# A recurrent memory kernel: the new memory summed over bands once, turned by a VectorE block transpose, its rows moved by DMA

## The chip, the cores and the metric

The kernel runs on one core of a Trainium2 chip. The metric is the device time of one execution in microseconds, lower is better; before the change three runs gave 1661.87 us as median, from 1659.44 to 1663.67. The engines are TensorE (PE, with its weight loads shown apart as PEld), VectorE (DVE), ScalarE (ACT), GpSimd (POOL) and SyncE (SP), which issues all DMA transfers of this kernel.

## The reference, cut to what matters

Two rounds of a memory-augmented attention (A) and a gated MLP (B) over 2048 tokens of width 448. In A the sequence is cut into 64 segments of 32 tokens. Each segment is preceded by 8 memory rows, all 16 heads (256 wide) attend over the 40 rows, and the first 8 output rows become the memory of the next segment, so the segments form a chain.

```python
for s in range(n_seg):
    xs = x[:, s * seg_len:(s + 1) * seg_len, :].copy()
    h = jnp.concatenate([mem, xs], axis=1)
    q, k, v = (jnp.einsum('btd,dhe->bhte', h, W) for W in (Wq, Wk, Wv))
    scores = jnp.where(mask, jnp.einsum('bhqe,bhke->bhqk', q, k) * scale, -1e9)
    o = jnp.einsum('bhqk,bhke->bhqe', _softmax(scores), v)
    o = jnp.einsum('bhte,hed->btd', o, Wo)
    mem = o[:, :M, :].copy()
    outs.append(o[:, M:, :])
...
x = x + _A_ref(_layernorm(x), mem0, ...)
x = x + _B_ref(_layernorm(x), W_gate, W_up, W_down)   # (relu(x Wg) * (x Wu)) Wd
x = x + _A_ref(_layernorm(x), mem0, ...)
x = x + _B_ref(_layernorm(x), W_gate, W_up, W_down)
```

## The kernel before, in words

The prologue loads Wq, Wk, Wv, Wo and folds them per head: A = Wq Wk^T with the scale, B = Wv Wo. Attention is then u = h A, scores = u h^T, softmax, y = P h, o = y B.

Two **chains** run side by side, one for each round of A, the second seven steps behind the first (`LAG`). A step (`chain`) takes both memories, 16 columns of `mT`, through one segment. Its instructions on TensorE are: u (L750, two halves of 56 matmuls in row and column tiles), the scores (L881), a transpose of the softmax (L914 from `Pm`), yy (L938 and L942 from `PTm` and `HR`) and oo (L785, 56 matmuls in four column tiles, one per band of 32 partitions). Between them VectorE and ScalarE evict, transpose u in blocks (L858, L866) and do the softmax. Another 16 columns of `mT` carry the tokens of odd tiles of the second round ("riders": boarded by GpSimd at L845 and L847, softmax from `Pr`, output gathered in `Tsb`).

The end of a step makes the new memory. oo leaves four partial sums, one per band. ScalarE rounds them to `Ohi` (L792), VectorE takes the rest as `Olo` (L793), GpSimd doubles 128 columns of each (L797). TensorE then forms the memory twice from the two: as columns, by 14 matmuls with `Ohi` or `Olo` as weights and a selector of 16 columns (L804), and as rows, by two matmuls of 448 columns with the selector as weights (L814). The columns are cast into `mT` for the next u and into `HT` for the next scores, the rows into `HR` (8 partitions, 384 and 64 columns for each chain), where yy reads them, and into `stage`, from which two transfers go to `Tsb`.

The **tiles** (128 tokens) are the other work: `norm` (layer norm; seven transposes at L972, evicted as 512 and 384 columns to `HT` and `HX`, or as 896 to `G2`; for attention eight transfers bring the rows to `HR`), `att_group` (L1021, L1046, L1093) and the MLP (L1115, L1133). 64 norms run in all, 32 for attention and 32 for the MLP.

The order is planned when the program is built. `_Sched` holds a list of operations with costs and makes each engine's instruction order by them, taking chain operations (`prio=0`) before tile work; in steps 0 to 4 it puts spinning matmuls (L1148) into gaps of TensorE. The array's tiling (`mode`) is switched as seldom as the plan allows. Every DMA has one of 48 semaphores in turn, in program order, so a transfer waits for the one 48 places earlier:

```python
if dma:
    n = len(self.dmas)
    o.slot = n
    if n >= self.N_DMA:
        o.deps[self.dmas[n - self.N_DMA]] = True
    self.dmas.append(o)
```

[...]

## Time and profile before

| What | us |
|---|---|
| median of three runs | 1661.87 |
| the profiled execution | 1664.92 |
| its span | 1662.8 |
| TensorE matmuls busy | 1599.4 |
| VectorE busy | 1167.1 |
| ScalarE busy | 842.1 |
| GpSimd busy | 95.3 |
| Spacing of two steps in the middle (oo at 841.55 and 860.44) | 18.9 |

The mean clock that TensorE was granted is 0.994. A line of the groups gives busy time and the mean duration of one instruction in ns, then the idle time of the engine in front of it and what ended that. In the timeline the first column is the start, the second the duration of a run of equal instructions. Matmuls are pipelined, so their pace is the distance of their starts. Busy time by stretch has the columns: stretch, its length, then busy time and instructions of PE, PEld, DVE, ACT and POOL, the granted clock, the DMA share and GB/s.

### The profile page before, as it was taken

How to read it: one execution, taken by the hardware profiler on the slowest of the kernel's cores; microseconds unless marked ns; L12 is line 12 of the kernel's file. 1: busy time of each engine (PE TensorE's matmuls, PEld its weight loads, DVE VectorE, ACT ScalarE, POOL GpSimd, SP SyncE). 2: the span in 40 equal slices, each digit the busy share in tenths (PEclk: the TensorE clock that was granted, in tenths of full speed). 3: DMA queues.
4: the chain of work that ended last, by engine and by line, in shares of the span. 5: the costliest groups of instructions: out<-in, count | busy, mean ns of one | idle time of the engine just before them, and what ended most of it. 6: DMA issues, size and time to landing. Idle time of an engine off the chain costs nothing.

```text
span 1662.8 us, 83559 instructions
## 1 busy us (share of the span) xinstructions
PE 1599.4 (96%) x38134; PEld 1123.4 (68%) x38134; DVE 1167.1 (70%) x3378; ACT 842.1 (51%) x2281; POOL 95.3 (6%) x342
## 2 busy tenths in 40 slices
PE   6999898999999999999999999999999999999997
PEld 4646565677676767766766776776867666767775
DVE  6646565777677777777677876786777777777563
ACT  5734344555555555545454554465455546444442
POOL 2000000000000000000000000000000000000000
PEclk9999999999999999999999999999999999999999
DMA  9350000000000000000000000000000000000000
GB/s 229 103 151 15 5 10 7 6 4 7 7 7 4 14 4 15 4 15 4 4 16 12 7 4 14 4 15 4 12 6 13 7 6 13 4 10 4 12 6 7
DMA packets 44976, 33.03 MB, mean 20 GB/s; under 512 B 17984, under 2 KB 43728, under 8 KB 44624
## 3 DMA queue, kind: packets, MB, share of 16 engines
q1 hardware_dynamic: 44624, 27.70, 6.4%
q8 instruction: 299, 4.90, 1.3%
q14 instruction: 53, 0.43, 0.1%
HBM read 21.36 MB, written 1.84 MB: 14 GB/s over the span
## 4 chain that ended last, share of the span: by engine, by line
PE 79%; DVE 11%; issue 4%; ACT 3%; SPq 2%; DMA 1%; POOL 0%; POOLq 0%; DVEq 0%
PE psG L1021 14%; PE psG L1093 12%; PE psC L785 10%; PE psG L1115 8%; PE psC L750 7%; PE psG L1133 3%; PE psG L750 3%; PE psG L632 3%; DVE uT L858 2%; PE psG L938 2%; SPq L594 2%; PE psG L1046 2%; PE psG L785 2%; PE psC L804 1%; PE psC L814 1%
## 5 line engine op out<-in xcount | busy, mean ns | idle before, releaser
L1093 PE MATMUL psG<-Bsb,YT 128*128 128x448 bf16 x1288 | 273.6, 352 | 3.6 <-DVE YT L349 1.8
L1021 PE MATMUL psG<-HT,A 64*128 64x128 bf16 x5196 | 270.2, 217 | 2.3 <-DVE Usb L349 0.8
L1021 PE MATMUL psG<-HX,A 64*128 64x128 bf16 x3897 | 231.6, 217 | 0.1
L346 ACT ACTIVATE Ug<-psG 64x128 bf16<-64x128 f32 (+2 forms) x454 | 159.4, 375 | 101.8 <-PE psG L1021 91.8
L1115 PE MATMUL psG<-G,glu 64*128 64x128 bf16 x6160 | 188.8, 217 | 3.3 <-DVE G L349 2.2
L1021 PEld LDWEIGHTS psG<-HT,A 64*128 64x128 bf16 x5196 | 181.9, 95 | 13.0 <-issue 4.5
L1115 PEld LDWEIGHTS psG<-G,glu 64*128 64x128 bf16 x6160 | 178.0, 95 | 14.2 <-issue 6.9
L785 PE MATMUL psC<-Bsb,YTm 128*32 128x448 bf16 x3360 | 173.1, 358 | 5.9 <-DVE YTm L349 4.0
L1093 PEld LDWEIGHTS psG<-Bsb,YT 128*128 128x128 bf16 x1288 | 115.2, 98 | 93.5 <-DVE YT L349 2.4
L750 PE MATMUL psG<-A,mT 64*32 64x448 bf16 x4088 | 163.3, 350 | 1.7 <-DVE mT L349 0.9
L858 DVE STREAM_TRANSPOSE uT<-Usb 128x384 bf16<-128x384 bf16 x280 | 156.0, 560 | 4.7 <-ACT Usb L346 0.2
L750 PE MATMUL psC<-A,mT 64*32 64x448 bf16 x3752 | 155.1, 350 | 0.8 <-ACT YT L346 0.4
L1021 PEld LDWEIGHTS psG<-HX,A 64*128 64x128 bf16 x3897 | 147.5, 95 | 0.2 <-issue 0.2
L349 DVE CAST Ug<-psG 64x128 bf16<-64x128 f32 (+2 forms) x287 | 118.3, 428 | 38.5 <-PE psG L1021 34.6
L785 PEld LDWEIGHTS psC<-Bsb,YTm 128*32 128x32 bf16 x3360 | 85.4, 98 | 77.5 <-DVE YTm L349 5.4
L1121 DVE TENSOR_TENSOR hG<-hG,psG 128x512 bf16<-128x512 bf16 (+1 forms) x125 | 75.4, 617 | 66.0 <-ACT hG L1120 65.4
L1120 ACT ACTIVATE hG<-psG 128x512 bf16<-128x512 f32 (+1 forms) x127 | 68.9, 542 | 103.9 <-PE psG L1115 100.4
L346 ACT ACTIVATE YT<-psG 128x448 bf16<-128x448 f32 x222 | 110.5, 548 | 20.9 <-PE psG L942 20.1
L750 PEld LDWEIGHTS psC<-A,mT 64*32 64x32 bf16 x3752 | 80.4, 92 | 59.5 <-DVE PTx L349 2.6
L349 DVE CAST Usb<-psG 128x448 bf16<-128x448 f32 x105 | 63.7, 606 | 60.6 <-PE psG L750 60.4
L346 ACT ACTIVATE Usb<-psC 128x448 bf16<-128x448 f32 x105 | 57.1, 544 | 85.9 <-PE psG L750 65.7
L750 PEld LDWEIGHTS psG<-A,mT 64*32 64x32 bf16 x4088 | 84.2, 92 | 22.3 <-DVE HT L349 4.4
(224 smaller groups left out, 2877.3 us busy)
## 6 DMA issues: line engine op xcount, KB each, us to landing
glu<-in_A_Wo_dram SPq DMA_DIRECT2D x8, 448.0 KB
Bsb<-in_A_Wq_dram SPq DMA_DIRECT2D x8, 384.0 KB
Bsb<-in_A_Wk_dram SPq DMA_DIRECT2D x8, 384.0 KB
glu<-in_A_Wv_dram SPq DMA_DIRECT2D x8, 384.0 KB
HR<-xn SPq DMA_DIRECT2D x128, 24.0 KB
HR<-xn SPq DMA_DIRECT2D x128, 4.0 KB
X<-in_A_x_dram SPq DMA_DIRECT2D x16, 112.0 KB
Tsb<-stage SPq DMA_DIRECT2D x112, 7.0 KB
```

The lines of the kernel that those rows point to most:

```text
L346: return E.activation(out, i, ACT.Copy, scale=1.0 if scale is None else scale)
L349: return E.tensor_copy(out, i)
L632: i = E.matmul(bk.ap()[row0:row0 + mn, 0:D], lhsT=lhs[:, et, m0:m0 + mn], rhs=rhs[:, et, :], start=(et == 0), stop=(et == 1), tile_positio ...
L750: i = E.matmul(ub[v].ap()[32 * j:32 * j + 32, 0:D], lhsT=self.mT[rw, b, :], rhs=cols, start=(b == 0), stop=(b == 6), tile_position=(64 * v ...
L785: x = E.matmul(bo.ap()[32 * j:32 * j + 32, 0:D], lhsT=self.YTm[:, q, :], rhs=self.Bsb[:, chunks[q], :], start=(i == 0), stop=(i == 13), ti ...
L858: self.s.add("dve", dv_cost(384), lambda E, e, out=out, hh=hh: E.transpose(out, heads[hh]), r=[("Usb", 2 * half + v) for v in range(2)], w ...
L1021: i = E.matmul(ub[v].ap()[:, 128 * n:128 * n + 128], lhsT=self.A[rw, b, a0:a0 + 128], rhs=HT[rw, b, :, 0:SEG] if b < 4 else HX[rw, b - 4, ...
L1093: i = E.matmul(bo.ap()[:, 0:D], lhsT=YT[:, c, :], rhs=self.Bsb[:, 14 * g + c, :], start=(g == 0 and c == 0), stop=(g == 3 and c == 13))
L1115: i_ = E.matmul(two[v].ap()[:, 128 * c:128 * c + 128], lhsT=self.Wgu[rw, b, f0:f0 + 128], rhs=G[rw, b, :], start=(b == 0), stop=(b == 6), ...
L1120: s.add("act", 145 + 0.82 * N, lambda E, e, dst=dst, z=two[0], N=N: E.activation(dst, z.ap()[:, 0:N], ACT.Relu), r=[two[0]], w=[("hG", i, q)])
L1121: s.add("dve", dv_cost(N), lambda E, e, z=two[1], N=N, dst=dst: E.tensor_tensor(dst, dst, z.ap()[:, 0:N], ALU.mult), r=[two[1]], w=[("hG", ...
L1133: i_ = E.matmul(bk.ap()[:, 0:D], lhsT=hG[:, c, :], rhs=self.Wd[:, c, :], start=(c == 0), stop=(c == NFC - 1))
```

## The change

The new memory is summed over the bands once, as rows only. Sixteen matmuls in four column tiles (32 output partitions each) use one selector `Sel` of 32 columns, which adds the four bands. The tiles differ in what they take: tiles 0 and 1 the even and odd 32-column pieces of all seven 64-column blocks in their order, tiles 2 and 3 the same with blocks 1/2, 3/4 and 5/6 exchanged. One eviction writes the result to `Rsb` (128 by 224, two buffers), and one VectorE transpose of 32 by 32 blocks turns it into `mT`, which is laid out as seven blocks of three groups of 16 columns: memory, riders, and a third that nobody reads. The `HT` columns are copied from `mT` by GpSimd, four copies a step. The `HR` rows are moved from `Rsb` by DMA, four transfers for each chain and step, and the riders' rows go from `Rsb` to `Tsb` in four where two went from `stage`.

A norm does four transposes, one of each pair of 64-column blocks; the three blocks that need the halves exchanged are written by two evictions of 384 columns on 64 partitions each, across the halves. The block order of the folded weights and of the MLP's weights follows (`WHOLE`, `CROSS`); the gate weights come in one transfer. The initial memory is loaded as rows and turned by the same transpose. The softmax transposes take 128 weight columns for 104. The diff, cut to its core:

```diff
-XW = 576
-BLOCK = (128, 256, 384, 0, 192, 320, 448)
-LOW = (1, 3, 5, 0, 2, 4, 6)
-UPP = (2, 4, 6, 0, 3, 5, 1)
+XW = 512
+BLOCK = (128, 256, 384, 0)
+LOW = (0, 1, 2, 3, 4, 5, 6)
+UPP = (0, 2, 1, 4, 3, 6, 5)
+WHOLE = (3, 0, None, 1, None, 2, None)
+CROSS = (None, None, 0, None, 1, None, 2)
...
-        spans = {"Wg0": (0, o1), "Wg1": (o1, 4 * F), "Wg2": (4 * F, o3), "Wu0": (0, o1), "Wu1": (o1, 4 * F), "Wu2": (4 * F, 6 * F),
-                 "Wu3": (6 * F, o3), "Wd": (o3, n)}
+        spans = {"Wg": (0, o3), "Wu0": (0, F), "Wu1": (F, o3), "Wu2": (F, o3), "Wd": (o3, n)}
...
-        m2 = self.mem0_d.rearrange("b a d -> d (b a)")
...
+        rows = self.mem0_d[0].rearrange("a (b s i) -> a s b i", s=2, i=32)
+        R = self.Rsb[0]
+        s.add("pool", 300, lambda E, e: E.memset(R[:, :], 0.0), w=[("R0", j) for j in range(10)])
...
+                self.dma(to[:, a], of[:, b], 3584, w=[("R0", n)])
...
-        for O, k in ((hi_, "Ohi"), (lo_, "Olo")):
-            c9 = O[:, :].rearrange("p (a d) -> p a d", d=64)
-            s.add("pool", 250, lambda E, e, c9=c9: E.tensor_copy(c9[:, 0:9:8], c9[:, 1:3]), r=[k], w=[k + "2"], **P)
...
-                for v, O in enumerate((hi_, lo_)):
-                    i = E.matmul(pk()[:, k, :], lhsT=O[:, BLOCK[k]:BLOCK[k] + 128], rhs=self.Sel16[:, :], start=(v == 0), stop=(v == 1))
...
-        s.add(EV, ev_cost(112), copy_any(self.mT[:, :, 0:16], pk), r=[bc_], w=["mTm"], **P)
...
+        R = self.Rsb[step % 2]
+        rk = ("Rsb", step % 2)
+        pieces = [[(0, 7, 1, 0)] if j < 2 else [(0, 1, 1, 0), (1, 3, 2, 2), (2, 3, 2, 1)] for j in range(4)]
 
         def rows(E, e):
-            for q, O in enumerate((hi_, lo_)):
-                i = E.matmul(br.ap()[0:104, 0:D], lhsT=self.SelR[v][:, 0:104], rhs=O[:, mid], start=(q == 0), stop=(q == 1))
-            return i
-        s.add("pe", mm_cost(D, D), rows, r=["Ohi", "Olo", ("SelR", v)], w=[br], alloc=[br], **P)
+            for i in range(3):
+                for q, O in enumerate((hi_, lo_)):
+                    for j in range(4):
+                        if i >= len(pieces[j]):
+                            continue
+                        to, n, st, of = pieces[j][i]
...
+                        x = E.matmul(dst, lhsT=self.Sel[:, :], rhs=src, start=(q == 0), stop=(q == 1), tile_position=(0, 32 * j))
+            return x
+        s.add("pe", 250, rows, r=["Ohi", "Olo", "Sel"], w=[br], alloc=[br], room=[rk], mode=1, **P)
+        s.add(EV, ev_cost(224), copy_any(R[:, :], lambda: br.ap()[:, 0:224]), r=[br], w=[rk], **P)
+        s.add("dve", dv_cost(224), lambda E, e: E.transpose(self.mT[:, :, 0:3:2, :], R[:, :].rearrange("p (b i) -> p b i", i=32)), r=[rk], w=MEM, **P)
         for c, sg, _ in act:
...
-            s.add(EV, ev_cost(32), copy_any(HT[:, :, n % 4, SEG:L], lambda c=c: pk()[:, 0:4, 8 * c:8 * c + 8]), r=[bc_], w=[("HTm", *key)], **P)
-            rw = slice(64 * (n % 2) + SEG, 64 * (n % 2) + L)
+            s.add("pool", 200, lambda E, e, c=c, HT=HT, n=n: E.tensor_copy(HT[:, 0:3, n % 4, SEG:L], self.mT[:, 1:7:2, 0, 8 * c:8 * c + 8]),
+                  r=[("mT", c)], w=[("HTm", *key, 0)], **P)
...
-            s.add(EV, ev_cost(384), copy_any(HR[rw, KM:KW], lambda rw=rw: br.ap()[rw, 64:D]), r=[br], w=[("HRm", *key)], **P)
-            s.add(EV, ev_cost(64), copy_any(HR[rw, KT:KT + 64], lambda rw=rw: br.ap()[rw, 0:64]), r=[br], w=[("HRt", *key)], **P)
+            for v in range(2):
+                src = R[32 * v + 8 * c:32 * v + 8 * c + M, :].rearrange("p (b i) -> p b i", i=32)
+                dst = HR[r0:r0 + M, KM:KW].rearrange("p (b s i) -> p b s i", s=2, i=32)[:, :, v]
+                self.dma(dst, src[:, 1:7], 3072, r=[rk], w=[("HRm", *key, v)], prio=0)
+                self.dma(HR[r0:r0 + M, KT + 32 * v:KT + 32 * v + 32], src[:, 0], 512, r=[rk], w=[("HRm", *key, 2 + v)], prio=0)
...
-            s.add("pe", mm_cost(*[128] * 7), tr, r=xnk + ["ident"], w=[bk], alloc=[bk], room=[("G2", g)])
-            s.add(EV, ev_cost(896, fast=True), copy_any(self.G2[g][:, :, :], pk), r=[bk], w=[("G2", g)])
+            s.add("pe", mm_cost(*[128] * 4), tr, r=xnk + ["ident"], w=[bk], alloc=[bk], room=[("G2", g, v) for v in range(3)])
+            s.add(EV, ev_cost(512, fast=True), copy_any(G[:, 0:4, :], pk), r=[bk], w=[("G2", g, 0)])
+            for v, to, of in ((1, lo, up), (2, up, lo)):
+                s.add(EV, ev_cost(384, fast=True), copy_any(G[to, 4:7, :], lambda of=of: pk()[of, 0:3]), r=[bk], w=[("G2", g, v)])
```

## The prediction, made before the changed kernel was run

> **What bounds the kernel now.** I read the page's head and busy times first, then the busy time by stretch of the span, then the two matmul groups that go, and last the timelines at the end of a step, in the prologue and on the DMA queue.

> ```profile
> span 1662.8 us, 83559 instructions
> PE 1599.4 (96%) x38134; PEld 1123.4 (68%) x38134; DVE 1167.1 (70%) x3378; ACT 842.1 (51%) x2281; POOL 95.3 (6%) x342
> ...
> PE 79%; DVE 11%; issue 4%; ACT 3%; SPq 2%; DMA 1%; POOL 0%; POOLq 0%; DVEq 0%
> ```
> TensorE is busy for 96% of the span and makes up 79% of the chain of work that ended last; every other engine has a quarter of the span or more to spare.

> ```profile
> 0.00:40.00 40.00, 27.33 (x297) 18.34 (x297) 25.33 (x63) 19.76 (x31) 9.33 (x28) 1.00 0.92 227
> ...
> 180.00:400.00 220.00, 203.13 (x5062) 141.44 (x5047) 152.89 (x444) 107.88 (x313) 11.89 (x43) 0.99 0.03 7
> 400.00:800.00 400.00, 391.87 (x9735) 276.71 (x9741) 298.13 (x896) 212.81 (x604) 24.07 (x89) 1.00 0.03 8
> 800.00:1200.00 400.00, 394.90 (x9884) 285.17 (x9872) 295.30 (x887) 209.37 (x586) 23.09 (x85) 1.00 0.04 9
> ```
> Of 63 us without a matmul, 12.7 lie in the first 40 and 16.9 between 180 and 400. From 400 on TensorE misses 1 to 2%. There the recurrent chain (u, scores, yy, oo, new memory) has tile work to fill its gaps, so removed TensorE time is gained, if the filling holds.

> ```profile
> L804 PE MATMUL psC<-Sel,Ohi 128*128 128x16 bf16 x476 | 40.8, 171 | 2.9 <-DVE Olo L793 2.9
> L972 PE MATMUL psG<-ident,xn 128*128 128x128 bf16 x434 | 35.3, 224 | 6.2 <-POOL xn L966 4.8 <-DVE Tx L1053 1.0 <-ACT Ug L346 0.3
> L814 PE MATMUL psC<-Ohi,SelR 128*104 128x448 bf16 x59 | 22.0, 372 | 0.0
> ```
> These durations include the time in the pipe. The pace is in the timeline, where I take starts, not durations:

> ```profile
> 796.25 0.17 PE L804 MATMUL psC<-Sel,Ohi 128*128 128x16 bf16 x1
> 796.27 0.17 PE L804 MATMUL psC<-Sel,Olo 128*128 128x16 bf16 x1
> ...
> 796.50 0.37 PE L814 MATMUL psC<-Ohi,SelR 128*104 128x448 bf16 x1
> ...
> 797.08 0.34 PE L938 MATMUL psG<-PTx,HR 40*128 40x128 bf16 x6
> ```

> **The change part by part.** *New memory on TensorE.* From 796.25 to 797.08 is 0.83 us per step for 14 column sums (25 ns each) and two row sums (about 0.2 each). They go, 70 times: -58.1. In their place stand 16 matmuls in four column tiles. Lower bound: 448 moving columns per tile at L814's 0.42 ns a column, 0.19 us. Upper bound, no overlap: 4 x 0.094 + 4 x 0.025 (L804's pace) + 8 x 0.040 = 0.79. The nearest row is oo, L785: 56 matmuls of 448 columns in four tiles run from 791.57 to 794.33, 2.7 us or 0.048 each, where one alone takes 0.19; the tiles overlap. [...] That is +21.0, net **-37** (bounds -45 to -3).

> [...]

> *Switches of the array's tiling.* L1021 (row tiles) hands over to L881 (none) at 785.28, where its pace of 28 ns from 785.02 would have ended at 785.19: about 0.1 us. Counted along both programs' TensorE order, switches go from 681 to 732: **+5**.

> *Norms.* Four transposes for seven, 64 times. L972's seven take 815.09 to 815.48, 0.056 each: 64 x 3 x 0.056 = **-11**. Their evictions become one of 512 and two of 384 columns on 64 partitions (ScalarE rows HT 0.60, HX 0.49) for one of 896 (0.92): up to 0.66 later when all are on ScalarE. 32 such norms feed an MLP, so 0 to +21; norms are issued ahead of a tile's other work, and now all of L1115 waits 3.3 us in total, so I take 0. Without that cover it is the 0.66 each.

> *Prologue.* Nine loads of the initial memory hold the DMA queue first; the first weights are issued at 8.16 and TensorE starts 4.6 us later:

> ```profile
> 0.74 6.24 SPq L594 DMA_DIRECT2D mT<-in_A_mem_dram  x9
> 7.02 1.10 SPq L594 DMA_DIRECT2D X<-in_A_x_dram  x2
> 8.16 0.97 SPq L594 DMA_DIRECT2D Bsb<-in_A_Wq_dram  x2
> ...
> 12.77 0.82 PE L615 MATMUL psG<-ident,Bsb 128*128 128x128 bf16 x6 [7.35 <-DMA Bsb<-in_A_Wq_dram]
> ```
> Afterwards these loads wait for GpSimd's zeroing and stand behind the x tiles and nine pairs of weight loads. Everything starts up to 6.3 us earlier; the identity, ready at 3.21, is in time. From 25 to 100 TensorE is full, so nothing swallows it: **-6** (0 to -6.3). The gate weights become one load that waits for all staging; MLP work comes some 50 us later.

> *VectorE, ScalarE, GpSimd.* Per step go a 0.27 cast of mT, two HT (0.18), two HR of 384 (0.48) and two of 64 columns (0.20) and the stage copy (0.53): 2.5 us. In come one eviction of 224 columns (0.36, between the 384- and 128-column rows) and one block transpose: L858 has 0.56 for 384, L866 0.42 for 256, so 0.39. Neither engine bounds; I book nothing. From Olo to the next u it was 108.05 to 109.38, 1.33; it becomes 0.05 + 0.30 + 0.21 + 0.36 + 0.06 + 0.39 + 0.05 = 1.42. That counts only in the dozen early steps where the chain is the bound (Ohi at 106.84, then at 122.72): **+1**. Four GpSimd copies (L847's 0.23 each) bring the HT columns 0.9 us after the transpose; scores come 5.9 us after u starts (109.38 to 115.25), which hides them. Uncovered they would cost 0.9 a step. The third boarding copy waits, as the two did, on GpSimd alone.

> *Rows by DMA.* This is the risk. Eight transfers a step (and four of Tsb for two) now stand on SP's queue, at 0.62 each as the Tsb row has it. Landing after the last issue starts:

> ```profile
> 1189.85 5.45 SPq L594 DMA_DIRECT2D HR<-xn  x8
> 1196.49 0.40 DVE L963 TENSOR_SCALAR xn<-X,lnst 128x448 bf16<-128x448 bf16 x1 [1.48 <-DMA HR<-xn]
> ```
> 1196.49 - (1195.30 - 0.62) = 1.8; the burst at 546.97 gives 2.9. In an ordinary step the last rows are there 0.6 (eviction, semaphore) + 7 x 0.62 + 2.9 = 7.8 us after the row sums; the TensorE work ordered between them and the next yy is at least 10.8 us (instructions times paces above). Hidden. But DMA number n waits for number n-48 in program order, and 66 are now issued per four steps where 26 were. In one step of four SP's order is: four rows of chain 1, four HR<-xn, four HR<-xn of the other layer, four HR<-xn, then four rows of chain 0, each of these last waiting for a landing of the HR<-xn just before. Twenty issues of 0.6 put the last landing at 0.6 + 11.5 + (1.8 to 2.9) plus up to 1.0 of waits: 13.9 to 16.0. The TensorE work in front of that yy is 13.1 to 13.9, with seven switches some 14.3. Late by 0 to 1.7, 11 times; I take 0.9: **+10** (0 to +60, if the norm's xn is itself late).

> Sum: -37 + 5 - 11 - 6 + 1 + 10 = -38. The profiled execution took 1664.9, so 1627; the median, 1661.9, lies 3 below the profiled one, so **1625**, with 1606 to 1648 as this case's own range.

> **Rivals.** (a) *TensorE's time comes back as idle time.* The re-made order fills worse, or the chain bounds more steps than it did. For it: 16.9 us idle from 180 to 400 already, and some steps lose filling work. Against: 1 to 2% idle afterwards, while non-chain work is half of TensorE's. At two thirds lost, 38 becomes 13: 1649.
> (b) *The column tiles run one after the other*, 0.79: 1625 + 34 = 1659, no change. L785's pace is against it; that the 16 are narrow and uneven is for it.
> (c) *Slower: the rows of chain 0 come late behind the ring of 48.* Place: yy in one step of four. Without the 10 booked the sum is -47, so from 47 / 11 = 4.3 us of lateness each it is a loss. SP takes its queue in order; should rows also sit behind the output store and the x load there, each waited for, 2 x 2.9 comes on top: 0.9 + 5.8 = 6.7, 11 x 6.7 - 47 = +27, 1689. For it: SP already waits on the store (14.6 us in all). Against: the store at 839.25 stood 9 us ahead of that step's memory.
> (d) *It doesn't do what it says:* the early weights gain nothing because their slots are freed by TensorE; 6 us, inside the ranges.

> **How the numbers follow.** Chances: forecast 0.64, (a) 0.13, (b) 0.07, (c) 0.16. A change under 0.3%, 5 us, can't be told from none. Faster: all of the forecast and 0.10 of (a), 0.74; within: most of (b), a little of (a), 0.09; slower: (c) and a little, 0.17. The range takes the unknown costs' bounds below (-45 for the tiles, 0 for the late rows: 1607) and (b) above: 1605 to 1666, leaving out (c) and a little at the bottom.

> **What would show it** (line numbers of the changed kernel). L796's 16 matmuls spanning 0.3 us in the timeline, and PE's busy time near 1560. First L615 near 6.5. L933 <-PTm waiting for a DMA HR<-Rsb about 1 us in every fourth step and hardly elsewhere. HT copies on GpSimd with no matmul waiting for them. I am wrong if TensorE idles over 30 us more than now, or if yy waits for DMA in ordinary steps.

## The result, and the profile after

The changed kernel takes 1686.12 us (median of 4 runs, 1683.64 to 1686.35), the kernel before 1660.98 beside it: ratio 1.0146, 95% interval 1.0129 to 1.0164. It is slower by 1.5%; 1625 was forecast, with a range to 1666.

Head, granted clock and chain of waits on the page of the changed kernel:

```profile
span 1684.5 us, 83993 instructions
PE 1577.3 (94%) x37948; PEld 1088.6 (65%) x37948; DVE 1173.6 (70%) x3294; ACT 790.6 (47%) x2087; POOL 99.2 (6%) x510
...
PEclk9999998999999999999999999999999999999999
...
PE 66%; SPq 11%; DVE 11%; DMA 6%; issue 4%; ACT 3%; POOL 0%; POOLq 0%; DVEq 0%
```

TensorE's busy time fell by 22 us, not by 40, and it now stands still for 107 us instead of 63. SP's queue and DMA, 3% of the chain before, are 17%.

Busy time by stretch, same columns as before the change (length, PE, PEld, DVE, ACT, POOL, clock, DMA share, GB/s):

```profile
0.00:40.00 40.00, 33.89 (x358) 22.30 (x360) 27.05 (x60) 24.64 (x39) 9.18 (x28) 1.00 0.90 257
...
180.00:400.00 220.00, 203.22 (x5090) 137.03 (x5092) 153.46 (x438) 100.70 (x281) 12.40 (x67) 0.96 0.04 8
400.00:800.00 400.00, 378.20 (x9509) 263.36 (x9503) 293.83 (x858) 194.52 (x537) 26.31 (x141) 0.99 0.05 9
800.00:1200.00 400.00, 377.00 (x9675) 269.62 (x9677) 293.30 (x852) 190.23 (x521) 24.91 (x134) 0.99 0.05 9
```

The first 40 us gained 6.6 us of TensorE time, as forecast. From 400 to 1200, where TensorE had missed 13 us, it now misses 45, and the clock column, 1.00 before, reads 0.99.

I split each profiled span in four. The granted clock in stretches of 5 us, times the busy time there, says how much of "busy" is only a slower clock; the rest of busy is called work; idle is what is left of the span.

| profiled execution | span | work | idle to 40 us | idle later | slower clock |
|---|---|---|---|---|---|
| before | 1662.8 | 1590.9 | 12.7 | 50.7 | 8.5 |
| changed | 1684.5 | 1551.0 | 6.1 | 101.1 | 26.3 |
| difference | +21.7 | -39.9 | -6.6 | +50.4 | +17.8 |

The work that the change takes away is nearly what was forecast (-43). It comes back as 50 us of standing still and 18 us of slower clock. The forecast's own sign of being wrong, over 30 us more idle time, has come: 44 us in all. What TensorE waits for:

```profile
PE psC L933 <- DMA HR<-Rsb: 21.1, 9, 3.5
PE psC L909 <- DVE Pm L894: 13.9, 13, 3.3
PE psG L1020 <- DVE Tr L898: 8.3, 8, 2.0
```

(us in total, times, longest). yy (L933) waits for the new rows, 9 times, up to 3.5 us. One such step on SP's queue, then on TensorE (start, duration, engine, line, operation, count):

```profile
928.97 2.94 SPq L576 DMA_DIRECT2D HR<-Rsb  x4
931.95 8.66 SPq L576 DMA_DIRECT2D HR<-xn  x12
940.65 2.95 SPq L576 DMA_DIRECT2D HR<-Rsb  x4
943.65 2.94 SPq L576 DMA_DIRECT2D Tsb<-Rsb  x4
```

```profile
944.69 0.51 PE L933 MATMUL psC<-PTm,HR 40*128 40x128 bf16 x6 [2.59 <-DMA HR<-Rsb]
```

From 928.97 to 943.60 SP issues 20 DMAs without a break: 14.6 us, 0.73 each. The rows of chain 0 stand last among them, behind twelve HR<-xn; yy goes on 1.8 us after the last one's issue starts (943.60 - 0.74 to 944.69).

The other waits are put down to VectorE. The same sort of burst, on SP, VectorE and TensorE:

```profile
1406.28 9.33 SPq L576 DMA_DIRECT2D HR<-xn  x12
```

```profile
1415.73 0.40 DVE L958 TENSOR_SCALAR xn<-X,lnst 128x448 bf16<-128x448 bf16 x1 [4.52 <-DMA HR<-xn]
...
1416.23 0.40 DVE L894 TENSOR_SCALAR Pm<-Tm,stm 128x40 bf16<-128x40 f32 x2
```

```profile
1416.69 0.29 PE L909 MATMUL psC<-ident,Pm 128*128 128x128 bf16 x1 [3.33 <-DVE Pm L894]
```

A norm's xn may be overwritten only when the HR<-xn that read it have landed; these are in the burst. VectorE kept its order here: Pm, whose input ScalarE had finished at 1411.64, stands behind xn until 1416.23, and TensorE behind Pm. "Waits for VectorE" was a DMA wait one step back. Of TensorE's stops of over 0.8 us, 13, of 20 us together, have in the 9 us before them a VectorE instruction that waited for a DMA (HR<-xn, Tsb<-Rsb, the x load). That is nearness in time, not a cause followed up stop by stop, and the same count finds 4 stops of 5 us in the kernel before. With L933's 21 and 1 more for HR<-xn it gives 37 to 42 of the 50 us.

Not all of the slower clock belongs to these stops. Between 180 and 300 us, where TensorE waits not for a DMA but for the chain (uT, Pm, Olo, mT), the granted clock is 0.93 against 0.99 before, 4.6 of the 17.8 us. The kernels below in which the late rows are cured, or not moved by DMA at all, show 0.93 and 0.94 there too.

### The profile page after: what moved, and what is told of

Same layout as the page of the kernel before. It is cut to its first block, busy times and chain, and to the rows that moved or that the text cites. A ratio compares the mean times of both kernels' runs of the same rounds, so it can differ in the third digit from the quotient of the medians.

```text
span 1684.5 us, 83993 instructions
## 1 busy us (share of the span) xinstructions
PE 1577.3 (94%) x37948; PEld 1088.6 (65%) x37948; DVE 1173.6 (70%) x3294; ACT 790.6 (47%) x2087; POOL 99.2 (6%) x510
## 4 chain that ended last, share of the span: by engine, by line
PE 66%; SPq 11%; DVE 11%; DMA 6%; issue 4%; ACT 3%; POOL 0%; POOLq 0%; DVEq 0%
PE psG L1020 11%; SPq L576 11%; PE psC L772 10%; PE psG L1114 10%; PE psG L1092 8%; PE psC L737 5%; PE psG L1132 4%; PE psG L614 3%; DMA HR<-xn 2%; PE psG L737 2%; PE psG L933 1%; PE psG L772 1%; DVE uT L853 1%; PE psG L1045 1%; PE psG L597 1%
## 5 line engine op out<-in xcount | busy, mean ns | idle before, releaser
L1020 PE MATMUL psG<-HT,A 64*128 64x128 bf16 x4968 | 295.0, 218 | 9.6 <-DVE Tr L898 8.3
L1020 PE MATMUL psG<-HX,A 64*128 64x128 bf16 x3726 | 285.8, 218 | 0.0
L1020 PEld LDWEIGHTS psG<-HT,A 64*128 64x128 bf16 x4968 | 243.0, 95 | 19.4 <-DVE Tr L898 10.2
L1020 PEld LDWEIGHTS psG<-HX,A 64*128 64x128 bf16 x3726 | 209.1, 95 | 0.0
L346 ACT ACTIVATE Ug<-psG 64x128 bf16<-64x128 f32 (+2 forms) x411 | 147.4, 377 | 117.9 <-PE psG L1020 90.7
L1114 PE MATMUL psG<-G,glu 64*128 64x128 bf16 x6272 | 190.4, 217 | 5.6 <-ACT G L346 4.7
L1114 PEld LDWEIGHTS psG<-G,glu 64*128 64x128 bf16 x6272 | 177.8, 95 | 19.0 <-issue 6.5
L737 PE MATMUL psC<-A,mT 64*32 64x448 bf16 x3864 | 140.3, 354 | 5.7 <-DVE lnst L953 2.7
L737 PE MATMUL psG<-A,mT 64*32 64x448 bf16 x3976 | 142.8, 354 | 0.8 <-DVE YTm L349 0.6
L346 ACT ACTIVATE YT<-psG 128x448 bf16<-128x448 f32 x202 | 101.9, 544 | 26.7 <-PE psG L937 26.2
L349 DVE CAST YT<-psG 128x448 bf16<-128x448 f32 x166 | 99.0, 610 | 20.5 <-PE psG L937 20.2
L737 PEld LDWEIGHTS psC<-A,mT 64*32 64x32 bf16 x3864 | 69.9, 93 | 56.6 <-issue 7.0
L346 ACT ACTIVATE Usb<-psC 128x448 bf16<-128x448 f32 x93 | 50.5, 543 | 97.7 <-PE psC L737 49.5
L1132 PE MATMUL psG<-glu,hG 128*128 128x448 bf16 x434 | 94.6, 352 | 0.0
```

The lines of the kernel that those rows point to most:

```text
L346: return E.activation(out, i, ACT.Copy, scale=1.0 if scale is None else scale)
L349: return E.tensor_copy(out, i)
L737: i = E.matmul(ub[v].ap()[32 * j:32 * j + 32, 0:D], lhsT=self.mT[rw, b, 0:2].rearrange("p a q -> p (a q)"), rhs=cols, start=(b == 0), stop ...
L1020: i = E.matmul(ub[v].ap()[:, 128 * n:128 * n + 128], lhsT=self.A[rw, b, a0:a0 + 128], rhs=HT[rw, WHOLE[b], :, 0:SEG] if CROSS[b] is None e ...
L1114: i_ = E.matmul(two[v].ap()[:, 128 * c:128 * c + 128], lhsT=self.Wgu[rw, b, f0:f0 + 128], rhs=G[rw, WHOLE[b] if CROSS[b] is None else 4 + ...
L1132: i_ = E.matmul(bk.ap()[:, 0:D], lhsT=hG[:, c, :], rhs=self.Wd[:, c, :], start=(c == 0), stop=(c == NFC - 1))
```

## The experiments

Each ran beside the kernel before; ratios are against it, with the 95% interval. No kernel leaves a part of the computation out. Theories A and B: the ring of 48, or SP's pace and order; C: not the DMAs at all.

### Ring, prices, rows by engine, a second queue

```diff
-    N_DMA = 48
+    N_DMA = 144
```

> The changed kernel with 144 DMA semaphores in place of 48, so that a DMA waits for the one 144 before it in program order; nothing is left out. In the changed kernel's trace (1686 us) TensorE waits 21.1 us for DMA HR<-Rsb, about 22 us for VectorE rows that themselves stood behind a VectorE instruction waiting for a DMA (xn for HR<-xn, X for Tsb<-Rsb), and the clock falls to 0.5 after such stops, which costs about 24 us more than before. Theory A (false waits: the ring of 48 holds the rows back): nearly all of this goes, 1686 - 21 - 20 - 20 = about 1625. Theory B (SP's own pace and order: 66 issues of 0.69 us per four steps, taken in order, whatever the ring): only the slot waits between issues go, perhaps 1 us in each late step, about 1670 to 1686, and L933 still waits for HR<-Rsb over 10 us. Theory C (not the DMAs: the longer chain and the re-made order fill worse): no change, 1680 to 1690.

1652.44 us, 0.9939 (0.9922 to 0.9956). L933's wait is down to 0.7 us. This looked like A; but the planner sees ring waits as dependences, so without them it also chose another order.

```diff
-        self.s.add("sp", 570, lambda E, e: E.dma_start(dst, src), r=r, w=w, dma=nbytes, prio=prio)
+        self.s.add("sp", 690, lambda E, e: E.dma_start(dst, src), r=r, w=w, dma=nbytes, prio=prio)
...
-                o.end = dma_free + 2000.0
+                o.end = dma_free + 2600.0
```

> The changed kernel with the planner's prices of a DMA raised to the measured ones: 690 ns to issue for 570, and 2600 ns to land for 2000; the work is the same, only the planned order differs. Theory A (ring): the ring still holds the rows back, but the plan knows of it (slot waits are dependences), so part goes: 1655 to 1680. Theory B (SP's pace, which the plan has too short by 66 x 0.12 = 8 us per four steps): the plan puts TensorE work in front of the late yy and the wait goes: about 1635, L933 <- HR<-Rsb below 5 us. Theory C: 1680 to 1690.

1657.15 us, 0.9972 (0.9954 to 0.9990): A's time, but with B's sign, since TensorE waits 1.0 us for rows although the ring is still 48. Idle time after 40 us is 80 us: in this plan too TensorE stands still more than before the change.

```diff
+        s.add("pe", mm_cost(D, D), whole, r=["Ohi", "Olo", ("SelR", v)], w=[b2], alloc=[b2], **P)
...
-                self.dma(dst, src[:, 1:7], 3072, r=[rk], w=[("HRm", *key, v)], prio=0)
+            s.add(EV, ev_cost(384), copy_any(HR[rw, KM:KW], lambda rw=rw: b2.ap()[rw, 64:D]), r=[b2], w=[("HRm", *key, 0), ("HRm", *key, 1)], **P)
```

> The changed kernel with its rows made as before: a two-matmul row sum into a second bank, ScalarE or VectorE copies into HR and stage, two DMAs for Tsb; columns, prologue and norms stay as changed. Nothing is left out. Costs about 70 x 0.4 = 28 us of TensorE. Theories A and B (the row DMAs are the loss): idle and clock as before the change, so 1661 - 46 (TensorE work that the changed kernel saved by its trace) + 28 = about 1643. Theory C (the loss lies in the rest): 1686 + 28 = about 1714.

1656.71 us, 0.9964 (0.9950 to 0.9978). C is out as the whole cause: without row DMAs the time falls by 29 us, though TensorE has 27 us more work (1578.5). This plan, too, is a newly made one. Against 1643 it is still 14 late: 6 us more idle after the first 40 than before the change, 3 of clock, and less work saved.

```diff
-                self.dma(H[64 * h:64 * h + SEG, KM:KW], xn[r0:r0 + SEG, 128:512], 24576, r=xnk, w=[("HRx", l, b, p, h)])
+                self.dma(H[64 * h:64 * h + SEG, KM:KW], xn[r0:r0 + SEG, 128:512], 24576, r=xnk, w=[("HRx", l, b, p, h)], q="act")
```

> As the run with 144 semaphores, and the 16 issues of HR<-xn per norm pair (256 in all) on ScalarE's queue in place of SP's. Theory A: as with 144 semaphores alone, about 1625, perhaps a few us worse, since ScalarE gives 256 x 0.69 = 177 us to issuing (it is busy 790 of 1684). Theory B: SP's issues fall from 66 to 50 per four steps (34 us for 45) and the rows no longer stand behind HR<-xn that wait for a norm: clearly faster than 144 alone, about 1630 where that is 1675. Theory C: no better than 1680.

1667.27 us, 1.0036 (1.0023 to 1.0049), worse than 144 alone. ScalarE's own queue becomes 5% of the chain, and TensorE waits for its results: L1114 for G 7.8 us (3.0 with 144 alone). B's hope for this cure fell; it says nothing against B as the cause.

### Same order, no ring

```diff
+        for o, d in self.planned:
+            del o.deps[d]
```

The list `planned` holds the waits of the ring of 48; they are there for the plan and go before the program is written.

> The changed kernel with every engine's order exactly as in the changed kernel, planned with the ring of 48, but run with 144 semaphores and without the waits for the DMA 48 before. So nothing moves; only those waits go. Theory A (the ring's false waits hold the rows): TensorE's wait for HR<-Rsb falls from 21 to below 5 us, 1650 to 1660. Theory B (in the planned order the rows stand behind HR<-xn, Tsb and x on SP's queue at 0.69 us each, and behind what these wait for): the wait stays above 12 us, 1672 to 1686; then the 34 us of the first run came from the other order that the plan took without the ring.

1683.98 us, 1.0155 (1.0114 to 1.0196): no better than the changed kernel. The wait is untouched:

```profile
PE psC L939 <- DMA HR<-Rsb: 21.6, 10, 3.1
```

(Its L939 is the changed kernel's L933.) A falls, and with it the ring as the cause: SP issues back to back and does not wait for slots at these places. The 34 us of the first run came from the order.

### Which price

The first or the second edit of the price diff above, alone, at a ring of 48.

> The changed kernel, ring of 48, with the planner's price of a DMA's issue alone raised, 570 to 690 ns; landing stays at 2000. In the late steps SP issues some 20 DMAs without a break at 0.69 us, which the plan books at 0.57: 2.4 us short, and TensorE waited 1.1 to 3.5 us there. Theory K (the issue price): TensorE's wait for HR<-Rsb falls below 5 us (21.1), 1650 to 1665. Rival L (the landing): above 12 us, 1675 to 1686.

> The changed kernel, ring of 48, with the landing price alone raised, 2000 to 2600 ns; issue stays at 570. In the trace TensorE goes on 1.7 to 1.9 us after the last row's issue starts, less than the 2.0 that the plan has already. Theory K: the extra 0.6 us covers a part of 2.4, the wait for HR<-Rsb stays at 8 to 18 us, 1665 to 1682. Rival L: below 5 us, 1650 to 1660.

Issue price alone: 1650.22 us, 0.9946 (0.9930 to 0.9961), TensorE waits 1.3 us for rows. Landing price alone: 1668.64, 1.0067 (1.0040 to 1.0095), 5.9 us. K's times hold (1650 to 1665 and 1665 to 1682); the second wait, 5.9 us, lies between K's 8 to 18 and L's 5. The plan books an issue at 0.57 us where SP takes 0.69 to 0.73, 2.4 to 3.2 us too little over 20 in a row, and puts yy just where it thinks that the rows have landed. The landing price buys a margin that covers a part.

How much of the 36 us is the price, and how much that a new order misses the bad places by chance, is not separated. The ring of 144 got rid of L933's wait at the old price as well, and the two prices together (1657.15) are 7 us slower than the issue price alone. A re-made order moves the time by that much, so a difference of this size between two plans is no proof of its cause.

### Ring and prices together; three xn buffers

Both diffs above at once, and then, at either price, a third xn and lnst:

> The changed kernel with 144 DMA semaphores and the planner's DMA prices at 690 and 2600 ns, both at once (1652 and 1657 us apart, 1686 without). Theory AB (ring and SP's pace both cost, and the rest of the loss is DMA too): the plan knows the true landings and is free of the ring: VectorE's waits for DMA (27 us with 144 alone) and TensorE's stops behind them go, about 1635 to 1642. Theory F (what is left is the fill: chain stages with no tile work ready, as the 184 us pattern of uT, Pm and Olo waits in the run with the prices alone shows): 1648 to 1655.

> The changed kernel with 144 DMA semaphores and three xn and lnst buffers in place of two, planner's prices as they were. With 144 alone VectorE waited 16.2 us, 7 times, for DMA HR<-xn to free xn, and TensorE stopped behind four of these (1.2, 1.4, 2.4, 2.7 us). Theory AB: these stops and some 5 us of clock go: about 1640. Theory F: 1650, as with 144 alone (1652).

> 144 semaphores, true DMA prices (690 and 2600 ns) and three xn buffers. With two buffers it was 1638; with three and the low prices 1675, 22 above the two-buffer kernel at the low prices. If the low prices are to blame (the plan spends whatever slack it is given, as it counts on landings that come later): 1630 to 1642. If a third buffer harms by itself (norms run earlier, and their HR<-xn stand before the rows): 1655 or more.

```diff
-        self.xn = [sb(f"xn{i}", [128, XW]) for i in range(2)]
+        self.xn = [sb(f"xn{i}", [128, XW]) for i in range(3)]
...
-        i = self.xi % 2
+        i = self.xi % 3
```

| ring of 144 | two xn | three xn |
|---|---|---|
| old prices | 1652.44, 0.9939 | 1674.87, 1.0072 (1.0049 to 1.0096) |
| 690 and 2600 | 1637.64, 0.9844 (0.9817 to 0.9872) | 1627.61, 0.9811 (0.9790 to 0.9832) |

A third buffer harms at the old prices and helps at the raised ones (1630 to 1642 was expected). At the old ones VectorE waits 26.8 us for HR<-xn, more than with two (16.2): it looks as if the plan spends the freedom on tighter places that the DMAs do not keep. With two buffers the ring and the prices together give theory AB's time (1635 to 1642). The third at the old prices fits neither theory's figure. The kernel with all three beats both kernels. The head of its page, and one step of its SP queue:

```profile
span 1625.5 us, 84089 instructions
PE 1562.2 (96%) x37959; PEld 1082.1 (67%) x37959; DVE 1154.5 (71%) x3263; ACT 793.7 (49%) x2118; POOL 99.4 (6%) x510
```

```profile
902.48 6.37 SPq L576 DMA_DIRECT2D HR<-Rsb  x8
908.89 5.76 SPq L576 DMA_DIRECT2D HR<-xn  x8
```

All eight rows now go ahead of HR<-xn, and in its list of waits L933 has none above 0.4 us for rows.

### Controls

> A control: the kernel before the change with 144 semaphores and the DMA prices of 690 and 2600 ns. It issues 26 DMAs in four steps and TensorE waits for no DMA after the start. If the gain of these two settings is the repair of the changed kernel's late DMAs: no change, 1655 to 1667. If they are better settings for any kernel of this kind: 1645 or less, and the 1638 of the changed kernel with them is in part not its own.

1649.34 us, 0.9947 (0.9929 to 0.9965): the kernel before gains 10 us from the two settings as well, between the two figures. So against a kernel planned alike the change is worth 0.9947 - 0.9844, 1.0% or 17 us, with two xn. By the medians it is 12 us, since the kernel before read 1662.3 beside the one and 1659.0 beside the other; 1628 has no such partner, as no run has the kernel before with a third xn.

> The kernel before the change with the row DMAs alone put on top: up to eight per step (four of 8 partitions x 6 runs of 64 B, four of 8 x 1 run), released by Olo as the rows are, into a spare buffer that nobody reads; the ring stays at 48, prices as they were. Nobody waits for these rows, so what is lost is lost by what stands behind them on SP or waits for a slot: HR<-xn, X loads, the output, Tsb<-stage. Theory I (half of the changed kernel's stops are VectorE's, behind xn and X that were late through SP): 1675 to 1690, VectorE's waits for DMA above 25 us (before 14). Theory J (only the late rows themselves cost): 1661 to 1666.

```diff
+        for i in range(4 * len(act)):
+            self.dma(dst, src, 512 * n, r=[("go", step % 2)], w=[("dly", i)], prio=0)
```

1660.04 us, 1.0007 (0.9992 to 1.0022). Theory I falls: eight more issues a step cost nothing where nobody needs the rows and the order leaves room. VectorE's wait for HR<-xn is 12.3 us, as it was. The load on SP alone is not the loss; the place of what is needed within it is.

### What a stop costs

Both kernels keep the planned order of the kernel before and delay yy by GpSimd memsets of a buffer that nobody uses.

```diff
+            for i in range(11):
+                s.add("pool", 10, lambda E, e: E.memset(self.dly[:, :], 0.0), r=[k_("P0"), k_("P1")] if i == 0 else (), w=["dly"], **P)
```

> The kernel before the change, its planned order untouched, with ten long stops put in: in every fourth step from 23 to 59 eleven GpSimd memsets of a spare 128x256 buffer (about 0.29 us each) run from the chain's Pm, and yy waits for the last; some 2.3 us of TensorE standing still, ten times. Theory G (a stop costs itself and then a lower clock: after the changed kernel's 3.48 us stop at 1232 us the granted clock was 0.5 for 6.6 us): 1661 + 23 + 10 x 1.7 to 3.3 = 1700 to 1715, clock near 0.98. Rival H (the clock falls in the changed kernel for another cause): 1661 + 23 = 1684 at 0.994.

> As the ten long stops, but twenty short ones, in every second step, with seven memsets: about 1.1 us each, the same total of some 23 us. In the changed kernel's trace stops of 1.3 to 2.0 us in dense work (800, 877, 1062, 1176 us) were followed by no lower clock. Theory G with a threshold: only the 23 us, about 1684, clock 0.99. Theory G without one: as much as the ten long stops or more, 1700 to 1720.

(`range(7)`, in every second step.)

Long stops: 1703.92 us, 1.0252 (1.0233 to 1.0270). Short ones: 1693.74, 1.0195 (1.0167 to 1.0223). By the same split of the span as above, the long ones added 26.8 us of idle time and 11.1 of slower clock, the short ones 20.9 and 3.1. That 3.1 is at the low end: the short-stop kernel's four executions had a granted clock of 0.987 to 0.992, and the profiled one is the fastest (1689.9). Its median lies between theory G's two figures, 1684 and 1700. A long stop (before, during, after; the clock is the third figure from the end):

```profile
648.67:651.67 3.00, 2.99 (x44) 1.68 (x40) 2.76 (x14) 2.18 (x8) 1.35 (x5) 1.00 0.03 8
651.67:654.73 3.06, 0.01 (x3) 0.01 (x2) 0.46 (x2) 0.12 (x1) 2.54 (x9) 0.87 0.00 0
654.73:662.73 8.00, 8.00 (x103) 4.23 (x104) 3.08 (x8) 2.83 (x6) 0.16 (x1) 0.62 0.11 31
```

Of the 9 stops of yy above 2 us in the long run, 8 were followed by a lower clock; of the 13 between 1.2 and 1.8 us in the short run, 5. Theory G holds and H falls. The length of a stop alone does not decide; the last section shows what does, for the most part.

### Does saved TensorE work still pay?

> The best kernel so far (144 semaphores, true prices, three xn; 1628) with each norm's four transposes issued twice, the second time over the same results, and planned so: 64 x 4 x 0.056 = 14 us more TensorE work. If TensorE work is what sets the time: 1628 + 14 = 1642. Theory F (saved work comes back as idle, since the chain's dry steps bound): added work goes partly into that idle, 1628 to 1636.

```diff
-            for k, o in enumerate(BLOCK):
+            for k, o in [*enumerate(BLOCK)] * 2:
```

> The kernel with engine-made rows (1657) with 144 semaphores and true prices: columns, norms and prologue as changed, rows by two matmuls and evictions, 28 us more TensorE work than with row DMAs (1638 at these settings with two xn). If work sets the time: 1638 + 28 = 1666, or 1647 by its own earlier time less the 10 us that these settings gave the kernel before. Theory F: 1640 to 1648, so that the row DMAs, even planned at their price, return only a part of the 28.

(The engine-made rows above, with the ring's and the prices' diffs.)

Doubled transposes: 1640.41 us, 0.9882 (0.9862 to 0.9902). That is 0.71% or 12 us above the best kernel, for 16.0 us more work in the profiles. Work mostly sets the time; theory F falls here. Engine-made rows: 1653.40, 0.9957 (0.9940 to 0.9974), 1.13% or 19 us (16 by the medians) above the row DMAs at the same settings, for 29.6 us more work. Planned at their price, the row DMAs pay, at half to two thirds of the work that they save.

## Why the prediction was wrong, point by point

*New memory on TensorE, -37, switches +5, norms -11.* Right: -43 forecast, -39.9 in the changed kernel's profile, -37 to -44 in the other orders of it (work of 1553.7 to 1546.6). The 16 matmuls:

```profile
952.98 0.27 PE L796 MATMUL psC<-Ohi,Sel 128*32 128x224 bf16 x4
953.03 0.18 PE L796 MATMUL psC<-Olo,Sel 128*32 128x32 bf16 x2
...
953.09 0.26 PE L796 MATMUL psC<-Olo,Sel 128*32 128x224 bf16 x4
...
953.18 0.21 PE L796 MATMUL psC<-Olo,Sel 128*32 128x96 bf16 x2
953.32 0.23 PE L933 MATMUL psG<-PTx,HR 40*128 40x128 bf16 x2
```

From the first start to the next matmul it is 0.34 us where 0.30 was taken, 3 us a run. The sixteen themselves start within 0.20 us, in each of the 70 steps, and the last pair takes 0.04 more at the pace of its likes. The remaining 0.10 fits the hand-over to matmuls of another tiling, which the 0.83 us of before contain as well (796.98 to 797.08) and the 0.30 left out. With 0.49 us saved a step the three terms come to -34 + 5 - 11 = -40, as measured. No run shows the way in which the sum came to 0.30; what the trace shows in its place is the 0.20 of the starts and the 0.34 to the next matmul. Nor do the starts keep the program's order: in each of the 70 steps the two `Olo` matmuls of 32 columns on column tiles 2 and 3 start 0.06 us ahead (here at 953.03) of the two of 224 columns on tiles 0 and 1 (953.09), which the program issues first. So in these steps the former were not held by the latter. Rival (b), 0.79, is out.

*Prologue, -6.* Right: -6.6; the first L597 runs at 5.49 (near 6.5 forecast). *HT copies on GpSimd:* no matmul waits for them. *Chain, +1:* in one dry step, from the first matmul of the new memory to u, 1.35 us (280.73 to 282.08) against 1.28 before (285.72 to 287.00): 0.07 more for 0.09 forecast.

*Rows by DMA, +10: the step that failed.* The place was right: yy in one step of four, 20 issues in a row, rows of chain 0 last. Three things were wrong in it.
- The price of an issue. The sum took 0.6; this burst runs at 0.73. With 0.6 + 19 x 0.73 + 1.8 = 16.3 against 14.3 of TensorE work it would have given 2.0 late, not 0.9; 2.3 was measured (21.1 / 9). The prediction had shown a burst itself, eight HR<-xn in 5.45 us or 0.68 each; with that and its two landing times the sum gives 1.0 to 2.1 late.
- Who else is hurt. It priced only yy's wait. Its bound of +60 named the other way, a norm's late xn, but neither the sum nor the range, which stops at 1666, took that in. The same bursts hold xn and Tsb, VectorE waits for these in order, and TensorE for VectorE: 15 to 20 us more.
- What a stop costs. It counted the stop alone. Long stops were followed by a lower clock (0.5 for 6.8 us at the one that ended at 1232.38): some 13 us more, which is the 17.8 without the 4.6 between 180 and 300 us.

By this count 22 + 15 to 20 + 13 makes 50 to 55 for 10 forecast: this term alone turns -38 into +2 to +7. The other 8 to 13 us of idle time, the 5 us of slower clock between 180 and 300 us and the 3 us less of saved work make up the rest of the +21.7. The forecast had nothing for these chain steps beyond its +1.

*Rival (c)* had the right side and, by luck, nearly the right time (1689), with the wrong mechanism: the ring and the output store do not hold the rows (the run in the same order without the ring), and it had no clock in it. *Rival (a)*, that saved time comes back as idle time, is not the main loss: in the best kernel idle time after 40 us is 56.9 (50.7 before) and the span is 37 below. That this is the forecast's sum is luck in part, since two of its three settings take 10 us off the kernel before as well. It keeps a part: against the kernel before at the same settings, 43 us less work with two xn gave 17 in the spans, with 24 more idle after 40 us (66.5 to 42.4) and 7 more of slower clock, in chain steps where uT, Pm or Olo is waited for with no tile work ready. Why the plan runs dry there was not tried.

## What to carry to other kernels

When a change swaps engine work for many small DMAs, price the issue on its queue from the longest burst in the trace, and look at what stands ahead of the needed transfer in that queue, not at the queue's load. A static plan with too low a price can turn a freedom into tighter places that are then missed: here the third buffer (1675), though not the larger ring (1652). Correct the price first. And when TensorE "waits for VectorE", look one step back for a VectorE instruction that was itself waiting for a DMA.

## What the runs showed of the hardware

In these runs a stop of TensorE could cost more than its length. The stop of 3.48 us that ended at 1232.38 in the changed kernel:

```profile
1227.79:1231.20 3.41, 1.11 (x18) 0.48 (x14) 1.32 (x4) 0.34 (x1) 0.00 (x0) 1.00 0.07 10
1231.20:1234.62 3.42, 2.24 (x48) 1.95 (x52) 1.36 (x3) 1.28 (x3) 0.00 (x0) 0.50 0.03 3
1234.62:1238.03 3.41, 3.41 (x44) 1.52 (x40) 1.05 (x4) 0.28 (x1) 0.00 (x0) 0.50 0.00 0
```

The granted clock is 0.5 from 1231.2 to 1238.0, 6.8 us, and TensorE loses about 3 us again. In the long-stop run the loss came in two sizes: a mean clock of 0.84 or 0.69 over the 11 us around a stop, 1.8 or 3.4 us.

Of the stops of 1.2 to 1.8 us five in thirteen were followed by a lower clock, of those of 2.2 to 3.3 us eight in nine: the length alone did not decide.

```profile
647.66:651.07 3.41, 2.17 (x16) 0.93 (x14) 2.42 (x11) 2.27 (x8) 1.89 (x7) 1.00 0.00 0
651.07:654.48 3.41, 2.98 (x74) 1.97 (x78) 2.13 (x6) 1.98 (x4) 0.28 (x1) 1.00 0.00 0
732.99:736.40 3.41, 1.62 (x42) 1.08 (x35) 2.25 (x7) 2.24 (x8) 1.87 (x6) 1.00 0.08 18
736.40:739.81 3.41, 2.83 (x17) 1.37 (x17) 1.55 (x3) 0.54 (x1) 0.60 (x3) 0.50 0.02 5
```

Both reach over the end of a step. The first leaves TensorE 2.17 and 2.98 us of work in its two steps, and the clock stays. The second, with 0.6 us of other idle time in front of it, leaves 1.62 us in the step where it begins, and the next step runs at 0.5. Counted over all eighteen traces without their first and last 40 us, a step at full clock with under 1.5 us of matmuls was followed by a lowered one 95 times in 95, with 1.5 to 2.1 us 41 times in 116, and with more 4 times in some 7,900. So in these traces a stop costs extra, for the most part, where it empties about half of one such step, alone or with other idle time near it.
